# A decode attention kernel: GpSimd's program six instructions shorter

## The chip, the cores and the metric

The kernel runs on one core of one Trainium2 chip. The metric is the device time of one execution in microseconds (us), the median of several executions. The profile of one execution also gives a span, from its first to its last recorded instruction. Here the span is about 1.8 us shorter than the device time. A run would be slow if it were over 1.5% above the fastest of its kernel. Differences of a few tenths of a microsecond matter here, a thousandth of the time, so each pair of kernels is timed in the same rounds.

## The reference

One query position attends over 65,536 keys. There are 32 query heads in groups of four, and each group shares one of 8 key and value heads:

```
B, Hq, Hkv, Sq, Sk, D = 1, 32, 8, 1, 65536, 128      # all bfloat16
k, v   = repeat(k, 4, axis=1), repeat(v, 4, axis=1)
scores = einsum("bhqd,bhkd->bhqk", q, k) * D ** -0.5
out    = einsum("bhqk,bhkd->bhqd", softmax(scores), v)
```

K and V together are 268.4 MB, and each byte is used once. The work is a stream from memory.

## The kernel before

SyncE issues all loads of K and V into three buffers of 8.4 MB each. VectorE transposes K in place, TensorE (PE) multiplies, ScalarE takes the exponential, PE multiplies by V. GpSimd zeroes some tiles at the start, hands out semaphore credits (increments of a counter on which another engine waits) and writes each head group's query columns into a block-diagonal weight tile. PE and VectorE run a loop over the 8 groups; the programs of the others, GpSimd's among them, are unrolled. These are the parts that the change touches (cuts marked `# ...`):

```python
ex = sb("ex", [P, 4, 512], bf16)            # exponentials, before their transpose
vs = sb("vs", [P, D + 2], fp32)
vy = sb("vy", [P, D, 4], fp32)
# ...
k_lo = [0, 64, 128, 192]
s_k = {(b, lo): sem(f"s_k{b}_{lo}") for b in range(2) for lo in k_lo}   # landed parts of K
# ...
GP.mark(gp.memset(wz[:, :, :], 0.0))        # GP.mark: increments GpSimd's own semaphore
GP.mark(gp.memset(vs[:, :], 0.0))
GP.mark(gp.memset(ex[:, :, :], 0.0))
GP.mark(gp.memset(vy[:, :, :], 0.0))
n = GP.mark(gp.memset(ident[:, :], 0.0))
GP.after(n)
p_ident = GP.mark(gp.affine_select(out=ident[:, :], # ... ones on the diagonal
gp.sem_inc(s_vd, 2)                         # initial credits
gp.sem_inc(s_cl, 1)
for s in (s_k[1, 64], s_k[1, 192]):
    gp.sem_inc(s, 16 * (G - 1))
gp.sem_inc(s_v[1], 16 * (2 * G - 3))
gp.sem_inc(s_v[2], 16)
DV.mark(dve.memset(acc[:, :], 0.0))
# ... at the end of the kernel, GpSimd's part
for g in range(G):
    if g == 0:
        GP.wait((s_dv, d_qT)); GP.after(p_ident)
    else:
        GP.wait((s_sc, 16 * g))
        gp.sem_inc(s_sd, 1)
        if g == 1:
            for t in k_lo[1:]:
                gp.sem_inc(s_k[0, t], 16 * (G - 1))
            gp.sem_inc(s_k[1, 128], 16 * (G - 2))
    for a in range(4):                      # four copies into the weight tile
        # ...
GP.wait((s_sc, 16 * G))
gp.sem_inc(s_sd, 1)
GP.wait((s_dv, d_sum(G)))
gp.sem_inc(s_w, 4)
```

The credits for K exist because VectorE takes 16 from four semaphores for every K buffer, one for each quarter, while most K buffers arrive as one transfer, which feeds only one of the four.

## Time and profile before

| | before |
|---|---|
| device time, first three runs | 629.55 us (629.36 to 629.75) |
| span of the profiled run | 627.7 us |
| data moved | 268.49 MB, mean 428 GB/s |
| busy: PE, VectorE (DVE), GpSimd (POOL) | 57%, 55%, 2% |

The first lines are the head of the page of the kernel before, its row of DMA activity (one digit for each fortieth of the span, 9 meaning 90% or more of the 16 DMA engines' time) and its table of DMA queues with packets, megabytes and share:

```profile
span 627.7 us, 7067 instructions
...
DMA  8999999999999999999999999999999999999996
...
DMA packets 7003, 268.49 MB, mean 428 GB/s; under 512 B 856, under 2 KB 1112, under 8 KB 1496
...
q1 hardware_dynamic: 6944, 268.45, 99.2%
q8 instruction: 1, 0.02, 0.0%
q14 instruction: 2, 0.02, 0.0%
q10 hardware_dynamic: 56, 0.01, 0.0%
```

The DMA row says what bounds the kernel. The engines are busy from the second slice on, and while the stream runs nothing that is done faster elsewhere can help unless it brings data sooner. Between 10 and 622 us the data packets take up the whole time of the 16 engines (q1 at 100.2% in the second table below), at 433 GB/s. The two q14 packets, kind "instruction", are taken here for pieces of the engines' programs being fetched.

The same table of the kernel before, restricted to 10 to 622 us, which is inside the stream, leaves one of the two:

```profile
DMA packets 6329, 264.88 MB, mean 433 GB/s; under 512 B 703, under 2 KB 703, under 8 KB 1017
...
q1 hardware_dynamic: 6328, 264.87, 100.2%
q14 instruction: 1, 0.01, 0.0%
```

The chain of waits at the end of the kernel before (start, duration, what the engine did or waited for):

```profile
609.01 12.42 DMA io<-in_v_dram
621.43 0.04 issue
621.48 1.03 PE acc L254 x6
...
622.53 1.80 PE pf L359 x28
...
624.89 0.36 ACT o L487
```

The chain leaves the DMA stream when rows 192 to 224 of the last V buffer land, at 621.43 us. PE and one ScalarE copy follow; then the result is stored. Whatever delays the landing delays the end: PE starts 0.05 us after it, at 621.48.

The timeline of GpSimd (POOL) at the start of the kernel before (start, duration, line, operation and tile; in brackets the idle time before it and who ended it):

```profile
1.52 0.21 POOL L187 MEMSET vs<- 128x130 f32 x1
1.67 1.81 POOL L188 MEMSET ex<- 128x2048 bf16 x1
3.41 0.52 POOL L189 MEMSET vy<- 128x512 f32 x1
3.88 0.20 POOL L190 MEMSET ident<- 128x128 f32 x1
4.33 0.29 POOL L192 TENSOR_SCALAR_AFFINE_SELECT ident<-ident 128x128 f32<-128x128 f32 x1 [0.24 <-POOL ident L190]
```

And VectorE (DVE) of the same kernel, as it comes to the first two K buffers:

```profile
6.48 0.69 DVE L384 TENSOR_REDUCE vs<-vy 128x128 f32<-128x512 f32 x1
8.50 4.45 DVE L373 STREAM_TRANSPOSE io<-io 128x4096 uint32<-128x4096 uint32 x1 [1.34 <-DVEq L119]
...
32.89 8.77 DVE L373 STREAM_TRANSPOSE io<-io 128x4096 uint32<-128x4096 uint32 x2 [5.11 <-DVEq L119]
```

VectorE is idle for 1.34 us before the first transpose of K, because the first 2 MB land at 8.36 us. GpSimd's zeroing is therefore off the path.

### The profile page before, as it was taken

The numbers are of one execution on the slowest core, as the hardware profiler recorded it, in microseconds if no ns is written. First come the engines' busy times: TensorE is split into PE (matmuls) and PEld (weight loads), VectorE is DVE, ScalarE is ACT, GpSimd is POOL, SyncE is SP. The second block draws the span as 40 slices with busy tenths as digits, with TensorE's granted clock in tenths as the row PEclk, the third lists the DMA queues.
The fourth block names the chain that finished last, engine by engine and source line by source line (L and its number), as shares of the span: only waits on it lengthen the run. The fifth ranks groups of instructions, "written<-read, shape, count | busy, mean of one in ns | idle before, by whom it ended". The sixth has DMA issues, their size and how long they took to land. (4 is left out here: it accounts for less than half of the span.)

```text
span 627.7 us, 7067 instructions
## 1 busy us (share of the span) xinstructions
PE 356.4 (57%) x2142; PEld 139.8 (22%) x2142; DVE 345.5 (55%) x154; ACT 34.4 (5%) x26; POOL 9.7 (2%) x42
## 2 busy tenths in 40 slices
PE   1865483827638275381844808458193571886346
PEld 0322131312213032130321303123031230332112
DVE  7795835649066490764807557084670946684210
ACT  0000100020000200002000020000200002000100
POOL 2000000000000000000000000000000000000000
PEclk9978595967959678596785958859587695899676
DMA  8999999999999999999999999999999999999996
GB/s 362 441 468 401 468 401 468 401 468 401 468 401 464 405 459 409 447 422 447 422 438 430 426 443 409 459 405 464 401 468 401 468 401 468 396 437 434 434 432 274
DMA packets 7003, 268.49 MB, mean 428 GB/s; under 512 B 856, under 2 KB 1112, under 8 KB 1496
## 3 DMA queue, kind: packets, MB, share of 16 engines
q1 hardware_dynamic: 6944, 268.45, 99.2%
q8 instruction: 1, 0.02, 0.0%
q14 instruction: 2, 0.02, 0.0%
q10 hardware_dynamic: 56, 0.01, 0.0%
HBM read 268.44 MB, written 0.01 MB: 428 GB/s over the span
## 5 line engine op out<-in xcount | busy, mean ns | idle before, releaser
L301 PE MATMUL acc<-io,wz 128*128 x1024 | 272.7, 420 | 184.8 <-PEq L119 157.3
L373 DVE STREAM_TRANSPOSE io<-io 128x4096 uint32<-128x4096 uint32 x64 | 279.9, 4416 | 157.2 <-DVEq L119 157.2
L301 PEld LDWEIGHTS acc<-io,wz 128*128 x1024 | 106.4, 104 | 351.2 <-issue 272.5
L254 PE MATMUL acc<-io,et 128*16 128x512 bf16 x1016 | 72.5, 416 | 19.3 <-PEq L119 19.2
L440 ACT ACTIVATE ex<-acc,nmb 128x2048 bf16<-128x2048 f32 x8 | 15.7, 1967 | 556.9 <-DVE nmb L420 556.9
L410 DVE TENSOR_REDUCE mg<-acc 128x1 f32<-128x2048 f32 x8 | 18.3, 2291 | 48.3 <-DVEq L119 48.3
L254 PEld LDWEIGHTS acc<-io,et 128*16 128x16 bf16 x1016 | 27.7, 94 | 58.4 <-issue 35.5
L248 PE MATMUL pf<-vs,sel 128*4 128x130 f32 (+1 forms) x20 | 5.7, 386 | 54.2 <-PEq L119 54.2
L376 DVE STREAM_TRANSPOSE et<-ex 128x1024 bf16<-128x1024 bf16 x17 | 20.8, 1225 | 22.6 <-SPq L154 12.8
L450 ACT ACTIVATE acc<-wz 128x2560 f32<-128x2560 bf16 (+2 forms) x8 | 16.3, 2040 | 1.0 <-ACT ex L440 0.2
L412 DVE TENSOR_REDUCE m<-pt 1x4 f32<-1x128 f32 x8 | 2.2, 279 | 22.7 <-DVEq L119 22.7
L514 POOL COPY wz<-qT 32x16 bf16<-32x16 bf16 x32 | 6.1, 189 | 512.6 <-PE acc L301 440.3
L248 PEld LDWEIGHTS pf<-vs,sel 128*4 128x4 f32 x20 | 1.2, 83 | 54.7 <-issue 54.6
L326 PE MATMUL pt<-et 128*16 128x512 bf16 x32 | 13.1, 411 | 0.0
L384 DVE TENSOR_REDUCE vs<-vy 128x128 f32<-128x512 f32 x9 | 6.1, 681 | 7.6 <-DVEq L119 7.6
L423 DVE TENSOR_TENSOR vy<-acc,sely 128x512 f32<-128x512 f32 x8 | 8.5, 1064 | 0.0
L472 DVE TENSOR_TENSOR vy<-acc,sely 128x512 f32<-128x512 f32 x1 | 0.7, 691 | 11.5 <-PE acc L254 11.5
L343 PE MATMUL pb<-ident,nrow 1*128 1x1 f32 x8 | 1.6, 194 | 7.5 <-PEq L119 7.5
L326 PEld LDWEIGHTS pt<-et 128*16 128x16 bf16 x32 | 3.1, 97 | 4.5 <-issue 1.4
L341 PE MATMUL pt<-ident,mg 128*1 128x128 f32 x8 | 2.3, 283 | 2.6 <-PEq L119 2.6
L420 DVE COPY nmb<-pb 128x1 f32<-128x1 f32 x8 | 1.3, 157 | 3.9 <-DVEq L119 3.9
L343 PEld LDWEIGHTS pb<-ident,nrow 1*128 1x128 f32 x8 | 1.1, 139 | 8.9 <-issue 8.9
(31 smaller groups left out, 22.8 us busy)
## 6 DMA issues: line engine op xcount, KB each, us to landing
io<-in_v_dram SPq DMA_DIRECT2D x5, 4096.0 KB, 16.9
io<-in_k_dram SPq DMA_DIRECT2D x8, 2048.0 KB, 27.4
io<-in_k_dram SPq DMA_DIRECT2D x2, 4096.0 KB, 34.4
io<-in_v_dram SPq DMA_DIRECT2D x1, 2048.0 KB, 10.3
io<-in_v_dram SPq DMA_DIRECT2D x1, 1024.0 KB, 12.4
io<-in_v_dram SPq DMA_DIRECT2D x3, 256.0 KB, 12.8
io<-in_v_dram SPq DMA_DIRECT2D x2, 128.0 KB, 12.8
io<-in_k_dram SPq DMA_DIRECT2D x13, 48.4
```

The source lines that it names most:

```text
L248: return pe.matmul(out=pf[0:H, 0:w], lhsT=sel[:, :], rhs=vs[:, 0:w], skip_group_check=True, **kw)
L254: return pe.matmul(out=vacc[32 * c:32 * c + 16, :, :], lhsT=et[:, ch // 2, w0:w0 + 16], rhs=io[:, PS * ch + 4 * tt:PS * ch + 4 * tt + 4, : ...
L301: i = pe.matmul(out=bass.AP(acc, r_o, [[2560, P], [1, 512]]), lhsT=bass.AP(wz, r_w + ((2 * s + e) * WB - 4 * u), [[4 * WB, P], [1, P]]), r ...
L326: pe.matmul(out=pt[0:16, :], lhsT=et[:, 0, 0:16], rhs=et[:, 0, :], start=True, stop=True)
L373: dve.transpose(out=part, in_=part).then_inc(s_kt, 2)
L376: dve.transpose(out=et[:, :, :].rearrange("p i n -> p (i n)"), in_=ex[:, 2 * b:2 * b + 2, :].rearrange("p i n -> p (i n)"),).then_inc(s_et, 1)
L384: DV.mark(dve.tensor_reduce(out=vs[:, 0:D], in_=vy[:, :, :], axis=AX.X, op=ALU.add))
L410: dve.tensor_reduce(out=mg[:, :], in_=sc, axis=AX.X, op=ALU.max).then_inc(s_mg, 1)
L423: dve.tensor_tensor(out=vy[:, :, :].rearrange("p d y -> p y d"), in0=vacc, in1=sely[:, :, None].to_broadcast([P, 4, D]), op=ALU.mult,).the ...
L440: act.activation(out=ex[:, :, :].rearrange("p b n -> p (b n)"), in_=sc, func=ACT.Exp, bias=nmb[:, :], scale=SCALE, accum_out=vs[:, D + g % ...
L450: act.activation(out=part, in_=wz[:, 0, 0:1].to_broadcast([P, part.shape[1]]), func=ACT.Copy).then_inc(s_cl, 1)
L514: gp.tensor_copy(out=wz[r, :, c0:c0 + H].rearrange("p (s w) h -> p s w h", s=2), in_=qTb[r, :, :, g, :],).then_inc(s_w, 1)
```

## The change

The intent is a shorter GpSimd program. The zeroed tiles become one allocation with one memset. The second and the fourth quarter of each K buffer share their semaphores with those of the other (the prediction calls them the upper halves). One credit rides on the memset, and another is given by VectorE.

```diff
-    ex = sb("ex", [P, 4, 512], bf16)
     et = sb("et", [P, 2, 512], bf16)
-    vs = sb("vs", [P, D + 2], fp32)
-    vy = sb("vy", [P, D, 4], fp32)
+    zs = sb("zs", [P, 1024 + 4 * D + D + 2], fp32)
+    ex = zs[:, 0:1024].bitcast(bf16).rearrange("p (b n) -> p b n", n=512)
+    vy = zs[:, 1024:1024 + 4 * D].rearrange("p (d y) -> p d y", y=4)
+    vs = zs[:, 1024 + 4 * D:]
@@
     s_k = {(b, lo): sem(f"s_k{b}_{lo}") for b in range(2) for lo in k_lo}
+    for lo in k_lo[1::2]:
+        s_k[1, lo] = s_k[0, lo]
@@
     GP.mark(gp.memset(wz[:, :, :], 0.0))
-    GP.mark(gp.memset(vs[:, :], 0.0))
-    GP.mark(gp.memset(ex[:, :, :], 0.0))
-    GP.mark(gp.memset(vy[:, :, :], 0.0))
+    gp.memset(zs[:, :], 0.0).then_inc(s_cl, 1)
@@
-    gp.sem_inc(s_vd, 2)
-    gp.sem_inc(s_cl, 1)
-
-    for s in (s_k[1, 64], s_k[1, 192]):
-        gp.sem_inc(s, 16 * (G - 1))
     gp.sem_inc(s_v[1], 16 * (2 * G - 3))
 
     gp.sem_inc(s_v[2], 16)
+
+    dve.sem_inc(s_vd, 2)
     DV.mark(dve.memset(acc[:, :], 0.0))
@@  (GpSimd's loop)
+            if g == 1:
+                GP.wait((s_sc, 8))
+                for t in k_lo[1::2]:
+                    gp.sem_inc(s_k[0, t], 16 * (2 * G - 2))
             GP.wait((s_sc, 16 * g))
             gp.sem_inc(s_sd, 1)
             if g == 1:
-                for t in k_lo[1:]:
-                    gp.sem_inc(s_k[0, t], 16 * (G - 1))
+                gp.sem_inc(s_k[0, 128], 16 * (G - 1))
                 gp.sem_inc(s_k[1, 128], 16 * (G - 2))
```

As built, GpSimd's program goes from 83 instructions to 77, and VectorE's from 72 to 73. The other engines' programs keep their lengths.

## The prediction

> **What bounds the kernel.** The DMA stream. The page's slice row shows the DMA engines at 9 tenths or more in all slices but the first two and the last; 268.4 MB move at 428 GB/s over 627.7 us. PE is busy 57%, DVE 55%, GpSimd 2%. The chain of waits at the end is DMA of V to 621.43 us, then 3.4 us of PE work, one ACT copy and the store of the output.

> **What the change removes, adds and moves.** Three memsets on GpSimd (vs 0.21, ex 1.81, vy 0.52 us in the timeline) become one of 1666 float32. From vy and ident (512 elements 0.52 us, 128 elements 0.20 us) I estimate 0.83 ns an element plus 0.1 us, so about 1.5 us: ident is ready some 0.9 us earlier. Four semaphore credits leave GpSimd's head (0.08 us each), one goes to VectorE. Two credits now come only after the eighth group of score matmuls (32.9 us) because the upper halves of both K buffers share a semaphore.

> **How much of that is on the path: none directly.** VectorE is ready for the first K at 7.2 us in the timeline and starts at 8.50, when the first 2 MB have landed (8.36); an earlier ident only widens this wait. The late credits are given at about 33.1 us; VectorE reaches the first transpose that needs one at 37.26.

> **The indirect part, which I think is the aim: instruction fetches.** The queue table has q14 "instruction" packets, 8 KB each. Restricted to 517 to 520 us it shows one among the data packets (started 518.16, 309 ns). The landing times of the 16 DMA engines show what it costs: up to 506 us the last engine lands 0.48 us after the first and 0.04 after the last but one; from 526 us on it is 0.78 and 0.29, to the end. So that fetch put one DMA engine 0.29 us behind for good, and every transfer waits for its last engine. [...] GpSimd is the likely owner: it ran its copies at 512.1 to 512.9 us[...]. (SyncE, issuing at 518.0, is the rival: then nothing changes.)

> All six dropped instructions precede that point, so the same fetch comes six instructions later in GpSimd's program: at its waits at 594.7 or 612.3 us (inside the stream: no gain) or after its final barrier wait ending 627.1 us (outside: 0.29 us gained). I give the last 65%.

> **Predicted time:** 629.3 us, range 628.9 to 629.8. Faster by over 2%: 1%; within 2%: 98%; slower by over 2%: 1%.

> **What would show each step.** Right: no 8 KB instruction packet between 10 and 624 us; the landings keep a spread of 0.48 us to the end; V's 192-to-224 chunk lands at about 621.1 instead of 621.43 and all after it moves alike; span about 627.4. One zs memset of about 1.5 us; VectorE's first K transpose still at 8.5; its second-half transpose of the second K still at about 37.3. Wrong: the packet still at 518 (another engine's), or at 597 to 618 with the spread opening there.

> **What would make it wrong.** The fetch is not GpSimd's, or only moves within the stream: then 629.5. VectorE's program is one longer and could pull in a fetch of its own late in the stream: then 629.5 to 629.8.  The chip's own scatter is 0.39 us over three runs, more than the gain.

The forecast's sum comes to 629.55 us (the first median of the kernel before) less the 0.29 us by which the last DMA engine lagged: 629.26, put down as 629.3.

## The result, and the profile after

| | before | after |
|---|---|---|
| device time, 6 runs each in the same rounds | 629.65 us (629.36 to 630.43) | 630.27 us (630.04 to 631.12) |
| ratio after to before, 95% interval | | 1.001 (0.9997 to 1.0023) |
| span of the profiled run | 627.7 us | 628.6 us |

A ratio here is the mean time of one kernel's fast runs over the mean time of the other's fast runs of the same rounds, so it is not quite the ratio of the medians quoted. By the interval the two kernels are the same within scatter. The medians are 0.62 us apart, and the prediction pointed the other way. The profiled pair is 0.83 us apart. That pair can be accounted for step by step.

The page of the changed kernel, head, DMA row and queue table:

```profile
span 628.6 us, 7062 instructions
...
DMA  8999999999999999999999999999999999999996
...
DMA packets 7002, 268.48 MB, mean 427 GB/s; under 512 B 856, under 2 KB 1112, under 8 KB 1496
...
q1 hardware_dynamic: 6944, 268.45, 99.1%
q8 instruction: 1, 0.02, 0.0%
q10 hardware_dynamic: 56, 0.01, 0.0%
q14 instruction: 1, 0.01, 0.0%
```

One q14 packet went away, as intended. But the count over the span does not tell which. The table restricted to 10 to 622 us, inside the stream, still has one:

```profile
DMA packets 6290, 264.78 MB, mean 433 GB/s; under 512 B 700, under 2 KB 700, under 8 KB 980
...
q1 hardware_dynamic: 6289, 264.77, 100.2%
q14 instruction: 1, 0.01, 0.0%
```

The packet that disappeared from the span is the one at 625.31 us, after the stream. The one in the stream stands at 597.43 us instead of 518.16. The trace's records go on past the span's end: there the kernel before has one 8 KB program packet, at 628.75 us, and the changed kernel two, at 628.67 and 629.58. So each has three from 10 us on, and what changed is where they fall.

The chain of waits at the end of the changed kernel:

```profile
609.64 12.46 DMA io<-in_v_dram
622.10 0.04 issue
622.15 1.02 PE acc L253 x5
...
623.20 1.78 PE pf L358 x28
...
625.56 0.36 ACT o L486
```

From the landing on, it is the chain of before with every piece about 0.67 us later. The delay is already there when the DMA lets go (622.10 against 621.43).

The start of GpSimd and of VectorE in the changed kernel, in two fences:

```profile
1.52 1.49 POOL L191 MEMSET zs<- 128x1666 f32 x1
2.95 0.20 POOL L192 MEMSET ident<- 128x128 f32 x1
3.40 0.29 POOL L194 TENSOR_SCALAR_AFFINE_SELECT ident<-ident 128x128 f32<-128x128 f32 x1 [0.24 <-POOL ident L192]
```

```profile
5.55 0.69 DVE L383 TENSOR_REDUCE zs<-zs 128x128 f32<-128x512 f32 x1
8.30 4.45 DVE L372 STREAM_TRANSPOSE io<-io 128x4096 uint32<-128x4096 uint32 x1 [2.07 <-DVEq L121]
...
32.65 8.77 DVE L372 STREAM_TRANSPOSE io<-io 128x4096 uint32<-128x4096 uint32 x2 [5.10 <-DVEq L121]
```

The merged memset takes 1.49 us, and the identity is ready 0.93 us earlier. Nothing of it is kept: VectorE's wait grows from 1.34 to 2.07 us, and its first transpose starts 0.20 us earlier only because the first 2 MB landed 0.20 us earlier in this profile (8.16 against 8.36 us). The late credits delay nothing either: the transposes of the second K buffer run as a pair of 8.77 us in both kernels.

What the views do not print is in the trace's records. Each transfer of K and V is done by all 16 DMA engines, and the time at which each of the 16 finishes is recorded. For the transfers named, this is how long after the last engine but one the last engine finished:

```
landing at about      506 us   526 us   594 us   604-605 us   V rows 192-224
before                 0.04     0.29     0.28       0.28       0.29 (lands 621.43)
after                  0.02     0.02     0.03       0.87       0.91 (lands 622.10)
```

So 15 of the 16 engines run as before (the last but one finishes that V part at 621.14 before and 621.19 after), and one engine is late from the first landing after the instruction packet on. In the kernel before its lag never closes: it is 0.27 to 0.29 us at every landing from 526 us to 622.79, and 0.22 to 0.26 in the last three small ones. The records do not name a packet's DMA engine, but these three packets of the changed kernel follow one another within 0.02 us and so are taken to be of one engine (start, end, ns, bytes, queue):

```
596.216  597.435   1219   32768   q1
597.432  597.764    332    8192   q14    program, not data
597.752  599.627   1875   32768   q1     the next data packet; its like take 1213 to 1224
```

The data engine gives 0.33 us to the program packet, and the data packet after it takes 0.66 us longer than usual: together about 0.98 us. At 518 us in the kernel before, among 64 KB packets, it was 0.31 us and 0.35 us (2769 ns instead of 2420), together about 0.65 us. At both places the program packet starts as a data packet ends (at 597.432 us with an end at 597.435, at 518.163 with one at 518.166). The data packet behind it is the only slow one of its size nearby: the other 64 KB packets of the kernel before take 2418 to 2429 ns between 400 and 525 us.

The sum for the profiled pair, before to after, is:

| step | before | after | difference |
|---|---|---|---|
| V rows 192 to 224 land | 621.43 | 622.10 | +0.67 |
| store of the output, issue to ScalarE seeing it done | 1.445 | 1.192 | -0.25 |
| GpSimd between two instructions of the final barrier | 0.078 | 0.444 | +0.37 |
| the rest (+0.053 us after that pause, -0.006 elsewhere; terms rounded) | | | +0.05 |
| span | 627.73 | 628.56 | +0.83 |

There are three unlike terms. The experiments have to say who fetched at 597 us, and what the pause in the barrier is.

### The profile page after: what moved, and what is told of

Read it like the earlier page. It is cut to its first block, busy times and chain, and to the rows that moved or that the text cites. A ratio compares the mean times of both kernels' runs of the same rounds, so it can differ in the third digit from the quotient of the medians.

```text
span 628.6 us, 7062 instructions
## 1 busy us (share of the span) xinstructions
PE 355.4 (57%) x2142; PEld 139.1 (22%) x2142; DVE 345.4 (55%) x154; ACT 34.4 (5%) x26; POOL 8.8 (1%) x40
## 5 line engine op out<-in xcount | busy, mean ns | idle before, releaser
L439 ACT ACTIVATE zs<-acc,nmb 128x2048 bf16<-128x2048 f32 x8 | 15.7, 1967 | 556.9 <-DVE nmb L419 556.9
L247 PE MATMUL pf<-zs,sel 128*4 128x130 f32 (+1 forms) x20 | 5.7, 386 | 53.3 <-PEq L121 53.3
L375 DVE STREAM_TRANSPOSE et<-zs 128x1024 bf16<-128x1024 bf16 x17 | 20.8, 1225 | 23.3 <-SPq L158 13.4
L383 DVE TENSOR_REDUCE zs<-zs 128x128 f32<-128x512 f32 x9 | 6.1, 681 | 7.6 <-DVEq L121 7.6
L422 DVE TENSOR_TENSOR zs<-acc,sely 128x512 f32<-128x512 f32 x8 | 8.5, 1064 | 0.0
L471 DVE TENSOR_TENSOR zs<-acc,sely 128x512 f32<-128x512 f32 x1 | 0.7, 690 | 11.6 <-PE acc L253 11.6
L204 DVE MEMSET acc<- 128x2560 f32 x1 | 2.2, 2192 | 1.7 <-SPq L64 1.7
```

Source lines behind the costliest of these rows:

```text
L247: return pe.matmul(out=pf[0:H, 0:w], lhsT=sel[:, :], rhs=vs[:, 0:w], skip_group_check=True, **kw)
L375: dve.transpose(out=et[:, :, :].rearrange("p i n -> p (i n)"), in_=ex[:, 2 * b:2 * b + 2, :].rearrange("p i n -> p (i n)"),).then_inc(s_et, 1)
L383: DV.mark(dve.tensor_reduce(out=vs[:, 0:D], in_=vy[:, :, :], axis=AX.X, op=ALU.add))
L422: dve.tensor_tensor(out=vy[:, :, :].rearrange("p d y -> p y d"), in0=vacc, in1=sely[:, :, None].to_broadcast([P, 4, D]), op=ALU.mult,).the ...
L439: act.activation(out=ex[:, :, :].rearrange("p b n -> p (b n)"), in_=sc, func=ACT.Exp, bias=nmb[:, :], scale=SCALE, accum_out=vs[:, D + g % ...
```

## The experiments

Ten runs were made, all correct, each in 5 rounds beside the kernel before. The table gives the readings of their profiles. "Packets" are the 8 KB program packets between 10 and 622 us; "lag" is that of the last DMA engine behind the last but one at V rows 192 to 224; "pause" is the time between two GpSimd instructions of the barrier (where all engines wait for one another at the end of the kernel; in the records of before and after the other four go on 0.04 to 0.05 us after GpSimd's second instruction), which is 0.08 us when nothing intervenes; "built" is the number of GpSimd and VectorE instructions.

| run | built | packets at us | lag us | pause us | span us | median us | before |
|---|---|---|---|---|---|---|---|
| before | 83, 72 | 518.16 | 0.29 | 0.08 | 627.7 | | |
| after | 77, 73 | 597.43 | 0.91 | 0.44 | 628.6 | 630.27 | 629.65 |
| pad6 | 83, 73 | 515.88, 598.43 | 0.24 | 0.08 | 627.9 | 629.80 | 629.54 |
| short6 | 77, 73 | 597.40 | 0.81 | 0.44 | 628.5 | 630.27 | 629.54 |
| out13 | 70, 73 | 597.27 | 0.88 | 0.08 | 628.0 | 630.16 | 629.54 |
| early5 | 88, 72 | 440.86 | 0.52 | 0.08 | 627.6 | 630.00 | 629.54 |
| dve72 | 77, 72 | none | 0.06 | 0.44 | 627.6 | 629.40 | 629.83 |
| dve73 | 83, 73 | 515.90, 598.59 | 0.40 | 0.08 | 628.0 | 629.90 | 629.83 |
| late_gp | 84, 72 | none | 0.04 | 0.08 | 627.2 | 629.05 | 629.83 |
| after2 | 77, 73 | 597.47 | 0.85 | 0.44 | 628.5 | 630.39 | 629.96 |
| late_gp2 | 84, 72 | none | 0.06 | 0.08 | 627.8 | 629.58 | 629.96 |
| before_late | 83, 72 | none | 0.00 | 0.08 | 627.9 | 629.76 | 629.96 |

The first theory was the prediction's own, with its losing branch come true: the packet at 597 us is GpSimd's, six instructions later than the one at 518. The rival was that some other part of the change costs the time.

### pad6: give GpSimd its six instructions back

```diff
+    for _ in range(6):
+        gp.sem_inc(s_pad, 1)
     gp.sem_inc(s_v[2], 16)
```

Expected:

> The changed kernel with six idle semaphore increments added back to GpSimd's head, so that its program is as long as before (83 instructions as built); all else of the change stays. Theory (the time depends on where GpSimd's next 8 KB of program is fetched): the instruction packet is back at about 518 us, beside 64 KB data packets, the landings open there by about 0.3 us, and the time is that of before, 629.4 to 629.9. Rival (one of the other parts, the single memset, the shared K semaphores, the credits or VectorE's longer program, costs the 0.6 us): the time stays at 630.1 to 630.6.

Measured: 629.80 us (629.78 to 629.83), ratio to before 1.0003 (0.999 to 1.0017). The time is the theory's. The picture is not. Its queue table inside the stream has two packets:

```profile
q1 hardware_dynamic: 6328, 264.86, 100.2%
q14 instruction: 2, 0.02, 0.0%
```

The GpSimd packet is back, at 515.88 us, but a packet at 598.43 us is there as well. The packet at 597 us is therefore not GpSimd's, and the theory in its first form fell although its time was right; that the time came out was luck. The only program that the change lengthened is VectorE's. The median is lower than the changed kernel's in spite of two packets, for two reasons that the table shows. The packets fall on different DMA engines (the lag jumps to 0.56 us at the first, and the second engine then ends only 0.24 us behind it), so the delays do not add. And the pause in the barrier is gone.

### short6: six GpSimd instructions fewer, nothing else of the change

```diff
-    GP.mark(gp.memset(wz[:, :, :], 0.0))      # and vs, ex, vy likewise
+    gp.memset(wz[:, :, :], 0.0).then_inc(s_v[1], 16 * (2 * G - 3))
+    gp.memset(vs[:, :], 0.0).then_inc(s_vd, 2)
+    gp.memset(ex[:, :, :], 0.0).then_inc(s_v[2], 16)
+    gp.memset(vy[:, :, :], 0.0).then_inc(s_cl, 1)
-    # the six sem_inc of GpSimd's head; two ride on VectorE's memset of acc and its sum for sel
```

Expected:

> The kernel before with six GpSimd instructions fewer and nothing else of the change: no merged memset and no shared K semaphores; the six initial credits ride on memsets and on two VectorE instructions. Theory: the fetch falls at about 597 us as in the changed kernel, one DMA engine is then late by 0.7 to 1.0 us to the end, and the time is that of the changed kernel, 630.0 to 630.6. Rival: the time stays that of before, 629.4 to 629.9.

Measured: 630.27 us (630.11 to 631.50), ratio 1.0014 (1.0001 to 1.0028), with a packet at 597.40 us. It copies the changed kernel without its merged memset and without its shared semaphores, so those are not the cause. It does not tell GpSimd from VectorE: as built, a wait that had ridden on one VectorE instruction became an instruction of its own, so VectorE's program was 73 long here too.

### out13: GpSimd thirteen shorter

```diff
-    GP.mark(gp.memset(wz[:, :, :], 0.0))
-    gp.memset(zs[:, :], 0.0).then_inc(s_cl, 1)
-    n = GP.mark(gp.memset(ident[:, :], 0.0))
+    gp.memset(wz[:, :, :], 0.0).then_inc(s_v[1], 16 * (2 * G - 3))
+    n = GP.mark(gp.memset(zs[:, :], 0.0))        # ident is now part of zs
-    # four sem_inc of group 1 leave GpSimd for ScalarE; s_cl and s_v[2] ride on VectorE's sums
```

Expected:

> GpSimd's program thirteen instructions shorter than before (zeroing of the identity in the same memset, two credits on other instructions, four credits moved to ScalarE). Theory: the fetch falls after GpSimd's wait in the final barrier, so no 8 KB instruction packet between 10 and 624 us, the spread of the landings stays as it starts (0.3 to 0.5 us), and the time is 0.3 us under before, 0.8 to 0.9 us under the changed kernel: 629.1 to 629.5. Rival (fetches do not matter): within 0.2 us of the changed kernel, 630.1 to 630.5. Risk: ScalarE's program is four longer and may pull in a fetch of its own.

Measured: 630.16 us (630.04 to 630.33), ratio 1.0009 (0.9995 to 1.0023): a clear miss. The time is that of the rival, "fetches do not matter"; what speaks against it is the lag of 0.88 us that opens at the packet. The packet stays at 597.27 us although GpSimd is seven instructions shorter than in the changed kernel. That is the second sign that it is not GpSimd's; VectorE's program was again 73 long. The pause in the barrier is absent, but the device time exceeds the span by 2.2 us here and by 1.8 to 1.9 in the other kernels. That would fit a pause that has moved behind the last recorded instruction. No view shows it, but a count of the records, given under late_gp, supports it.

### early5: GpSimd five longer

```diff
+    for _ in range(5):
+        gp.sem_inc(s_pad, 1)
     gp.sem_inc(s_v[2], 16)                   # in the kernel before
```

Expected:

> The kernel before with five idle semaphore increments more on GpSimd, so the fetch comes one group of heads earlier, at about 440 us, again among 64 KB data packets. Theory: the spread of the landings opens at 440 us rather than at 518 and stays; the cost is about that of before, so 629.4 to 629.9. If it is larger or smaller, by the packet that follows the fetch and by how early that engine was, the cost is a matter of place, not of the packet kind alone. Rival: no landing shifts at 440.

Measured: 630.00 us (629.44 to 630.31), ratio 1.0007 (0.9993 to 1.002), a median 0.1 us above the range expected. GpSimd executes five instructions for each group, and five more of them move the packet from 518.16 to 440.86 us, which is one group of 77.3 us. The lag opens at the next landing (0.07 us at 429 us, 0.46 at 449) and stays. The packet at 518 us of the kernel before is GpSimd's: that part of the prediction is shown, and its rival, SyncE, is out. (The records do not name the engine that fetches; a packet is assigned here by the program on whose length its place depends.) The packet cost more than at 518 us, 0.52 against 0.29 at the end. The fetch and the 64 KB data packet behind it take the same time in both kernels (309 and 2769 ns), so what is left to differ is how far ahead of the last engine that engine happened to be; this is the author's estimate, since no view names the engine.

The theory was now this: VectorE's one added instruction pulls VectorE's fetch from 625 us into the stream; GpSimd's fetch did leave the stream; and its price at the new place is the pause of 0.37 us in the barrier, which all engines wait for.

### dve72: the changed kernel with VectorE at its old length

```diff
-    dve.sem_inc(s_vd, 2)
-    DV.mark(dve.memset(acc[:, :], 0.0))
+    dve.memset(acc[:, :], 0.0).then_inc(s_vd, 2)
```

Expected:

> The changed kernel with one VectorE instruction fewer: the two initial credits ride on VectorE's zeroing of the accumulators, so that its program is as long as before (72 as built); GpSimd stays six shorter. Theory, formed from the four runs before: the packet at 597 us in the changed kernel is VectorE's, pulled in by its one added instruction, while GpSimd's own had left the stream. Then no instruction packet of 8 KB between 10 and 624 us, VectorE's is at about 625 as before, the landings keep their first spread of 0.3 to 0.5 us, the pause of 0.37 us in GpSimd's last barrier stays, and the time is 629.2 to 629.6. Rival (the packet is GpSimd's, moved from 518): it stays at 597 and the time at 630.1 to 630.5.

Measured: 629.40 us (629.26 to 630.23), ratio 0.9993 (0.9979 to 1.0007). The queue table inside the stream has no line for q14 any more:

```profile
DMA packets 6349, 264.85 MB, mean 433 GB/s; under 512 B 704, under 2 KB 704, under 8 KB 1042
...
q1 hardware_dynamic: 6349, 264.85, 100.2%
```

A packet is back after the stream, at 624.83 us; the lag is 0.06 us; V rows 192 to 224 land at 620.96 us instead of 622.10. One instruction made that difference. The pause stayed at 0.44 us, as expected.

### dve73: the kernel before with one idle VectorE instruction

```diff
+    dve.sem_inc(s_pad, 1)
     DV.mark(dve.memset(acc[:, :], 0.0))
```

Expected:

> The kernel before with one idle semaphore increment more on VectorE and nothing else. Theory (VectorE's fetch): two instruction packets in the stream, at about 518 (GpSimd's) and 597 (VectorE's, with the 32 KB packet after it 0.66 us longer), none at 625; the last landing is 0.2 to 0.6 us later than before and the time 629.7 to 630.2. Rival: only the packet at 518, time as before.

Measured: 629.90 us (629.61 to 630.19), beside 629.83 for the kernel before, ratio 0.9998 (0.9984 to 1.0011). The records are as expected: packets at 515.90 and 598.59 us, none at 625, and the last V transfer lands at 624.66 instead of 624.11. The time hardly answers. In the profiled pair the span grows by 0.30 us, not by 0.55: the store of the output takes 1.187 us instead of 1.445 from issue to seen. In the kernel before, VectorE's packet starts at 625.31 us, just after that store is issued at 625.28, and dve72 is alike (624.83, 624.81, and 1.388 us for the store). Where the packet starts 0.35 us before the issue (early5), or is nowhere near, the store takes 1.18 to 1.19 us; in late_gp below, with packets 0.28 and 0.13 us before the issue, 1.24. So that packet seems not to be free at its old place either; this is a coincidence in time across the profiles, not an experiment on the store.

pad6 and dve73 are also a pair: the same program lengths, and the same places of both packets, one with all the other parts of the change and one with none. They were run at other times. The medians are 629.80 and 629.90 us, and the ratios to the kernel before 1.0003 and 0.9998.

### late_gp: let GpSimd ask after the stream and before the barrier

```diff
-    GP.mark(gp.memset(wz[:, :, :], 0.0))
+    gp.memset(wz[:, :, :], 0.0).then_inc(s_v[1], 16 * (2 * G - 3))
-    gp.sem_inc(s_v[1], 16 * (2 * G - 3))
     # VectorE as in dve72; at the end of GpSimd's program:
     gp.sem_inc(s_w, 4)
+    GP.wait((s_dv, d_last))
+    for _ in range(8):
+        gp.sem_inc(s_pad, 1)
```

Expected:

> As the run with VectorE at its old length, but GpSimd, one instruction shorter still at its head, ends with a wait for VectorE's last sum (about 624 us) and eight idle increments, so that the point at which it asks for its next 8 KB comes after the stream and before the last barrier. Theory: GpSimd's packet shows at 624.5 to 626 us, nothing in the stream, and the pause of 0.37 us is gone from the barrier: 628.8 to 629.3, the fastest so far. Rival: the pause has nothing to do with the fetch and stays, with a time as the run without the added tail; or the fetch is asked for at 595 us while GpSimd waits, and the landings open there.

Measured: 629.05 us (628.89 to 629.87), ratio 0.9987 (0.9974 to 1.0001), the fastest kernel, 0.35 us under dve72. GpSimd's instructions in the trace's records:

```
dve72     barrier:          626.590  627.029  627.115 ...        (gap 0.44, then 0.09)
late_gp   idle increments:  623.325  623.403  623.481  623.560  623.999  624.082 ...
          barrier:          626.603  626.681  626.762 ...        (gap 0.08, 0.08)
```

The pause moved out of the barrier and into the idle increments, where nobody waits for GpSimd. Two packets follow, at 624.70 and 624.85 us. So the pause goes with a point in GpSimd's program; with it where nobody waits for GpSimd, as here, the median is 629.05 us, and 629.40 in dve72.

That this is the point at which GpSimd asks for more program is supported by a count of the records. In all seven profiles with a visible pause (after, short6, dve72, late_gp and the three below) it follows the 68th recorded GpSimd instruction. In the kernel before, the 68th is a copy at 512.76 us, after which GpSimd waits for VectorE until 523.13, so that no pause can show; the packet at 518.16 falls in this wait. In early5 the 68th comes at 435.26, before the packet at 440.86. out13 has only 67 recorded GpSimd instructions, so its pause would come after the last of them.

### after2, late_gp2 and before_late

after2 is the changed kernel and late_gp2 is late_gp, unedited. before_late has nothing of the change:

```diff
-    GP.mark(gp.memset(wz[:, :, :], 0.0))      # and vs, ex, vy: four credits ride on these
+    gp.memset(wz[:, :, :], 0.0).then_inc(s_v[1], 16 * (2 * G - 3))
@@
     gp.sem_inc(s_w, 4)
+    GP.wait((s_dv, d_last))
+    for _ in range(4):
+        gp.sem_inc(s_pad, 1)
```

Expected:

> The changed kernel again, to be compared on one chip with the two kernels beside it. All theories: within 0.3 us of its first 630.27 us, with the packet at 597 us, the last engine 0.8 to 0.9 us behind the last but one from there on, and the pause of 0.37 us in GpSimd's last barrier.

> The fastest kernel so far again. Theory (the changed kernel loses by two fetches, VectorE's in the stream and GpSimd's in the barrier): 1.0 to 1.4 us under the changed kernel of the same call, 0.5 to 0.9 us under the kernel before. Rival (the difference seen first was the chip's scatter): within 0.3 us of the kernel before.

> The kernel before, nothing of the change in it: four of GpSimd's initial credits ride on its memsets, and its program ends with a wait for VectorE's last sum and four idle increments, so it is as long as before (83) but asks for its next 8 KB after the stream. Theory (only the place of the fetches counts; the merged memset, the shared K semaphores and the earlier identity are worth nothing): no packet between 10 and 624 us, no pause in the barrier, and the time is that of the run beside it with the changed kernel's parts, 628.8 to 629.3. Rival (part of the gain is from the merged memset or the shared semaphores): 0.2 us or more above it.

Measured: after2 630.39 us (630.08 to 631.37), ratio to before 1.001 (0.9996 to 1.0023); late_gp2 629.58 us (628.85 to 629.80), ratio 0.9991 (0.9977 to 1.0004); before_late 629.76 us (629.67 to 629.88), ratio 0.9998 (0.9984 to 1.0011). The records of all three were as expected. They were run on another chip. The gain over the changed kernel was 0.8 us, less than the 1.0 to 1.4 expected; over the kernel before it was 0.4 instead of 0.5 to 0.9. before_late missed its range by 0.5 us, and stood 0.18 us above late_gp2, just under the 0.2 us that its rival asked for.

A reason can be read from late_gp and late_gp2, which are the same kernel. The DMA let go equally early (the last V transfer landed at 623.79 and at 623.69), but the profiled spans are 627.2 and 627.8. These lines give, for 621.5 to 624.0 us of late_gp, late_gp2 and before_late in this order, the length of the stretch, then busy time and number of instructions of PE, PE's weight loads, VectorE, ScalarE and GpSimd, the granted clock of PE, and the DMA share and rate:

```profile
621.50:624.00 2.50, 2.30 (x40) 1.72 (x33) 1.47 (x4) 0.00 (x0) 0.00 (x0) 1.00 0.69 235
```

```profile
621.50:624.00 2.50, 2.50 (x30) 2.21 (x23) 1.48 (x4) 0.00 (x0) 0.00 (x0) 0.50 0.67 228
```

```profile
621.50:624.00 2.50, 2.50 (x30) 2.21 (x23) 1.47 (x4) 0.00 (x0) 0.00 (x0) 0.50 0.70 236
```

PE ran the tail at full clock in the first (granted clock 1.00) and at half clock in the other two (0.50). In the records the small matmuls of the tail then start every 107 ns instead of every 56. The chain of late_gp2 shows where the 0.6 us are, in PE rather than in DMA:

```profile
608.15 12.84 DMA io<-in_v_dram
...
622.08 2.59 PE pf L356 x28
...
625.22 0.36 ACT o L484
```

Those 28 matmuls took 1.80 us in the kernel before. The clock records of before and after, 38 stretches in each, hold just these two values, 1.00 and 0.50. So this kernel has a second source of scatter of about 0.6 us. The stretch from the landing of V rows 192 to 224 to the store's issue gives its size: 4.62 and 4.70 us in late_gp2 and before_late, and 3.8 to 3.9 in the other ten profiles. Those ten hold tails at full clock and tails that reach it early: after and after2, with a mean of 0.62 and 1.00 between 621.5 and 624 us, took 3.84 and 3.81. So only a tail that stays at half clock to about 624 us is seen to cost.

At the same tail clock the two profiles agree: late_gp2 629.58 us and before_late 629.70, with the step to full clock at 624.1 and 624.3. With what pad6 and dve73 say, the other parts of the change seem worth no more than about 0.1 us. This rests on two pairs of profiles. All five runs of before_late lie between 629.67 and 629.88 us, while two of the five of late_gp2 are below 629.0; whether before_late always ends at half clock, and why, is not known, since one run of it was profiled.

The two calls of late_gp have medians 0.78 and 0.38 us under the kernel before, and each 95% interval just reaches 1. It is the fastest kernel in the median, but a gain of one thousandth is not proven by the times alone; its packets and lags are shown.

## Why the prediction was right or wrong

- **The bound, and the worth of the direct parts: right.** The DMA stream bounds the kernel (100.2% of the 16 engines' time from 10 to 622 us, before and after). The merged memset took 1.49 us (estimate 1.5), the identity came 0.93 us earlier (0.9), and nothing of it arrived. VectorE's transposes of the second K buffer stayed a pair of 8.77 us.
- **The mechanism: right.** A program fetch put a DMA engine behind for good (by 0.29 us from 526 us on in the kernel before, by 0.87 to 0.91 from 605 us to V rows 192 to 224 in the changed one). The packet at 518 us was GpSimd's (early5), and with six instructions fewer it left the stream (dve72: no packet, lag 0.06 us). That was the branch given 65%. In the four profiles with six instructions fewer (after, short6, dve72, after2) an 8 KB packet starts 0.1 to 0.3 us after the end of the span, where the other profiles with a GpSimd packet in the stream have none.
- **What failed first: "VectorE's program is one longer and could pull in a fetch of its own late in the stream: then 629.5 to 629.8."** This stood among the things that would make the prediction wrong and had no part in the 629.3 us, but it is what happened. dve72 and dve73 show it from both sides. Its size was wrong too: the time given for it is 0.2 to 0.5 us above the forecast, about what the lag of 0.29 us from the fetch at 518 us would cost. At 597 us, among 32 KB packets, it cost its engine 0.98 us, and the lag was 0.91.
- **What failed second: the step "after its final barrier wait ending 627.1 us (outside: 0.29 us gained)".** A fetch outside the stream was counted as free. At that place GpSimd pauses 0.37 us in the barrier, and the end of the kernel waits for it. dve72 has the pause and late_gp has not, at 0.35 us in the median. So even with VectorE's fetch held back, most of the gain was given back by this pause: in dve72 V rows 192 to 224 land 0.48 us earlier than in the kernel before, and the profiled span is only 0.11 us shorter.
- **A trap in the check that the prediction had set itself.** It said that a packet at 597 to 618 us would mean that GpSimd's fetch only moved within the stream. The packet came at 597 and was another engine's. pad6 and out13 were needed to see that.

Three things stay open. One is why one instruction moves VectorE's fetch by about 27 us (597 to 599 against 625 us), past some ten instructions. Another is why the data packet behind a fetch is slower, by 0.35 us at 64 KB and 0.66 at 32 KB. The third is whether the store of the output is really slowed by a fetch beside it.
